# Summing V accumulators through a mask on VectorE and one fp32 matmul, instead of a chain of eight

## The chip, the core and the metric

One core of a Trainium2 chip. The metric is the device time of one execution in microseconds (us).

Engine names: PE is the matmul engine, PEld its weight loads, DVE is VectorE, ACT is ScalarE, SP is the engine that issues the loads. "DMA engines" are the core's 16 engines that carry data.

## The reference

One query token attends to 65,536 keys, with 32 query heads and 8 key/value heads (4 query heads share one, which the kernel calls a group), head size 128, bf16:

```python
B, Hq, Hkv, Sq, Sk, D = 1, 32, 8, 1, 65536, 128
# q [B,Hq,Sq,D], k and v [B,Hkv,Sk,D], all normal * 0.05
k = jnp.repeat(k, Hq // Hkv, axis=1); v = jnp.repeat(v, Hq // Hkv, axis=1)
scores = jnp.einsum("bhqd,bhkd->bhqk", q, k) * D ** -0.5
p = softmax(scores)
return jnp.einsum("bhqk,bhkd->bhqd", p, v)
```

K and V together are 268.4 MB, every byte of which is read once.

## The kernel before

SP loads 64 tiles of 4 MB (128 partitions of 32 KB each) through five buffers, K of the next group in turn with V of the current one. For K, DVE transposes a tile and PE multiplies it with the query. For V, one accumulator row block serves four column slots, so that a matmul can be 32 columns by 512:

```python
def v_step(g, j):
    vt = load(v_view[g, j], "vt")
    # ... A = two PSUM accumulators of [128, 512] fp32, E = exp(scores), transposed
    for c0 in range(0, CW, NQ):
        for u in range(2):
            for s in range(NQ):
                c = c0 + s
                nc.tensor.matmul(out=A[u][s * QP:(s + 1) * QP, :], lhsT=E[:, j, c, :],
                                 rhs=vt_v[:, u, c, :, :], start=..., stop=...)
```

Most of A is not wanted: of each 32 rows, only the four of the block that belongs to the column's slot i (the "diagonal") count. The old kernel copies A to SBUF and gathers the diagonal blocks with fp32 matmuls against columns of a selection matrix:

```python
def collect(g, stop):
    A = A_tiles.pop(g)
    # ... As[0] <- A[0] on ACT, As[1] <- A[1] on DVE
    for i in range(NI):                                   # NI = 8
        nc.tensor.matmul(out=ps_f, lhsT=sel[:, i * HPG:(i + 1) * HPG],
                         rhs=As[i // HI][:, i % HI, :], start=(i == 0), stop=...)
```

The trace records 16 fp32 matmuls per group for these eight calls, two for each. The very last V tile is loaded in five pieces (1/2, 1/4, 1/8, 1/16, 1/16) and multiplied slot by slot in a narrow form (4 by 128), so that little work is left when its last piece lands:

```python
ps_f = collect(g, False)
for t in range(EDGE):                                      # EDGE = 120 of 128 slots
    s = t % NQ
    slot(t, Dp[s * QP:s * QP + HPG, :], t < NQ, t >= EDGE - NQ)
nc.vector.tensor_copy(out=Ds, in_=Dp)
for t in range(EDGE, T):                                   # the last 8 slots
    slot(t, ps_f[:, :], False, False)
nc.tensor.matmul(out=ps_f, lhsT=selh, rhs=Ds, start=False, stop=True)
store(g, ps_f, nc.sync)                                    # o = ps_f / sum, then the store
```

## Time and profile before

| | before |
|---|---|
| device time, median of 3 | 635.4 us (635.21 to 635.79) |
| span of the profiled run | 633.2 us |
| bytes loaded, mean rate | 268.4 MB, 425 GB/s |
| busy: PE, DVE, ACT | 62%, 54%, 4% |
| matmul records on PE | 2314 |
| last load landed, then to the end | 629.63 us, 3.6 us |

The first view is the page of the profiled run: the share of time in which the 16 DMA engines are busy and the rate, in 40 slices of the span; then the DMA queues with packets, megabytes and share of the engines' time.

```profile
DMA  8999999999999999999999999999999999999995
GB/s 366 433 433 436 435 432 433 430 433 427 439 427 433 431 430 431 432 433 431 430 429 430 431 432 431 430 431 431 432 431 430 431 434 433 432 431 431 430 423 233
...
q1 hardware_dynamic: 9800, 268.44, 98.7%
q8 instruction: 18, 0.29, 0.2%
```

The DMA engines are at 90% or more in nearly every slice, and the rate stands at about 430 GB/s until the last two slices (423 and 233). The second queue, 18 packets with 0.2% of the engines' time, carries the instructions of an engine's program.

The second view is the end of the chain of waits (start, duration, what):

```profile
598.94 30.69 DMA vt<-in_v_dram
...
629.68 0.67 PE ps_f L239 x8
630.34 0.44 PE ps_f L252 x2
...
630.81 0.34 DVE o L226
```

One load is waited for until 629.63 us. Eight slots, one matmul and the scaling of the output follow.

The third view is the table of stretches (start:end, length, busy time and count of PE, PEld, DVE, ACT and POOL, the granted clock of PE, DMA share, GB/s).

```profile
624.00:625.00 1.00, 1.00 (x12) 0.80 (x10) 0.07 (x1) 0.00 (x0) 0.00 (x0) 1.00 0.87 348
625.00:626.00 1.00, 1.00 (x60) 0.92 (x57) 0.00 (x0) 0.00 (x0) 0.00 (x0) 1.00 0.55 225
626.00:627.00 1.00, 0.44 (x25) 0.31 (x15) 0.00 (x0) 0.00 (x0) 0.00 (x0) 1.00 0.56 219
627.00:628.00 1.00, 0.62 (x32) 0.47 (x32) 0.00 (x0) 0.00 (x0) 0.00 (x0) 1.00 0.41 154
628.00:628.50 0.50, 0.13 (x12) 0.13 (x15) 0.00 (x0) 0.00 (x0) 0.00 (x0) 1.00 0.06 25
628.50:629.00 0.50, 0.26 (x16) 0.12 (x9) 0.00 (x0) 0.00 (x0) 0.00 (x0) 1.00 0.18 57
```

The fourth view is the timeline of the last tile (start, busy time, engine, line, operation, count, idle time before it and who ended that):

```profile
625.28 1.16 PE L239 MATMUL Dp<-vt,E 128*4 128x128 bf16 x58
627.11 0.62 PE L239 MATMUL Dp<-vt,E 128*4 128x128 bf16 x32 [0.67 <-DMA vt<-in_v_dram]
...
628.37 0.40 PE L239 MATMUL Dp<-vt,E 128*4 128x128 bf16 x16 [0.64 <-DMA vt<-in_v_dram]
...
629.68 0.67 PE L239 MATMUL ps_f<-vt,E 128*4 128x128 bf16 x8 [0.36 <-DMA vt<-in_v_dram]
```

PE has done the first half of the tile at 626.44 (625.28 + 1.16) and waits for each later piece.

### The profile page before, as it was taken

What the parts mean: (1) busy time and instruction counts of PE and PEld (TensorE: products, weight loads), DVE (VectorE), ACT (ScalarE), POOL (GpSimd) and SP (SyncE); (2) the same over time, 40 slices, a digit from 0 to 9 for tenths busy, and PEclk for the clock granted to TensorE, in tenths of its full rate; (3) what the DMA queues carried; (4) which work ended last, traced back from release to release, by engine and by line L of the source; (5) the groups of instructions that cost most, each with busy time, mean ns of one, the idle gap of its engine ahead of it and who ended that gap; (6) DMA issues with size and microseconds to landing.
All of it is one profiled execution on the core that took longest, in us unless ns stands there. A gap on an engine that the chain in (4) does not pass through costs nothing.

```text
span 633.2 us, 5208 instructions
## 1 busy us (share of the span) xinstructions
PE 395.6 (62%) x2314; PEld 158.3 (25%) x2314; DVE 341.7 (54%) x214; ACT 22.4 (4%) x25; POOL 4.9 (1%) x7
## 2 busy tenths in 40 slices
PE   0586776767457675587744777557774568654735
PEld 0232222222122221233211232122331223211313
DVE  0898663765437663466633666345754466553600
ACT  0000100010000100001000000001000010000100
POOL 3000000000000000000000000000000000000000
PEclk9999699758887588885868858688586898777977
DMA  8999999999999999999999999999999999999995
GB/s 366 433 433 436 435 432 433 430 433 427 439 427 433 431 430 431 432 433 431 430 429 430 431 432 431 430 431 431 432 431 430 431 434 433 432 431 431 430 423 233
DMA packets 10070, 268.81 MB, mean 425 GB/s; under 512 B 1344, under 2 KB 1344, under 8 KB 1728
## 3 DMA queue, kind: packets, MB, share of 16 engines
q1 hardware_dynamic: 9800, 268.44, 98.7%
q8 instruction: 18, 0.29, 0.2%
q10 hardware_dynamic: 248, 0.04, 0.0%
q14 instruction: 4, 0.03, 0.0%
HBM read 268.47 MB, written 0.01 MB: 424 GB/s over the span
## 4 chain that ended last, share of the span: by engine, by line
DMA 58%; PE 22%; DVE 15%; issue 5%; ACT 0%; ACTq 0%; DVEq 0%
DMA kt<-in_k_dram 44%; PE S L137 16%; DMA vt<-in_v_dram 12%; DVE kT L128 12%; DMA q_85<-in_q_dram 2%; PE ps_f L217 2%; DVE mx L148 2%; ACT ET L168 0%; PE ps_b L163 0%; DVE Z L112 0%; DVE o L226 0%; PE ps_t L150 0%; PE A_357 L201 0%; PE A_356 L201 0%; ACTq L77 0%
## 5 line engine op out<-in xcount | busy, mean ns | idle before, releaser
L137 PE MATMUL S<-kT,Z 128*128 128x512 bf16 x1024 | 296.7, 448 | 184.6 <-DVE kT L128 184.4
L128 DVE STREAM_TRANSPOSE kT<-kt 128x2048 int32<-128x2048 int32 x128 | 289.6, 2293 | 196.0 <-DMA kt<-in_k_dram 152.2
L137 PEld LDWEIGHTS <-Z 128*128 128x128 bf16 x1024 | 111.6, 109 | 368.3 <-issue 294.4
L201 PEld LDWEIGHTS <-E 128*32 128x32 bf16 x992 | 26.3, 100 | 48.7 <-issue 28.5
L173 DVE STREAM_TRANSPOSE E<-ET 128x2048 bf16<-128x2048 bf16 x8 | 18.5, 2311 | 17.4 <-ACT ET L168 17.4
L148 DVE TENSOR_REDUCE mx<-S 128x1 f32<-128x2048 f32 x8 | 18.3, 2292 | 15.9 <-PE S L137 15.9
L168 ACT ACTIVATE ET<-S,nm 128x2048 bf16<-128x2048 f32 x8 | 15.7, 1967 | 77.8 <-DVE nm L165 77.8
L201 PE MATMUL A_2721<-vt,E 128*32 128x512 bf16 x48 | 8.0, 584 | 12.0 <-DMA vt<-in_v_dram 12.0
L176 PE MATMUL ps_l<-ls,selh 128*4 128x1 f32 x16 | 1.5, 165 | 19.2 <-ACT ET L168 19.2
L214 DVE COPY As_2832<-A_2722 128x512 f32<-128x512 f32 x1 | 0.7, 693 | 21.0 <-PE A_2722 L201 21.0
L163 PE MATMUL ps_b<-one,mrow 1*128 1x1 f32 x16 | 3.2, 269 | 10.7 <-DVE mrow L157 10.7
L102 DVE STREAM_TRANSPOSE qT<-q_85 128x64 int32<-128x64 int32 x1 | 0.2, 245 | 16.0 <-DMA q_85<-in_q_dram 16.0
L226 DVE TENSOR_SCALAR o<-ps_f,rl 4x128 bf16<-4x128 f32 x8 | 2.7, 339 | 9.9 <-PE ps_f L217 8.8
L201 PE MATMUL A_2722<-vt,E 128*32 128x512 bf16 x48 | 7.9, 584 | 0.0
L201 PE MATMUL A_357<-vt,E 128*32 128x512 bf16 x64 | 7.1, 380 | 0.0
L201 PE MATMUL A_356<-vt,E 128*32 128x512 bf16 x64 | 6.9, 382 | 0.0
L201 PE MATMUL A_1045<-vt,E 128*32 128x512 bf16 x64 | 6.6, 380 | 0.0
L201 PE MATMUL A_2421<-vt,E 128*32 128x512 bf16 x64 | 6.6, 380 | 0.0
L201 PE MATMUL A_1733<-vt,E 128*32 128x512 bf16 x64 | 6.6, 380 | 0.0
L201 PE MATMUL A_701<-vt,E 128*32 128x512 bf16 x64 | 6.6, 380 | 0.0
L201 PE MATMUL A_1389<-vt,E 128*32 128x512 bf16 x64 | 6.6, 380 | 0.0
L201 PE MATMUL A_2077<-vt,E 128*32 128x512 bf16 x64 | 6.6, 380 | 0.0
(95 smaller groups left out, 119.1 us busy)
## 6 DMA issues: line engine op xcount, KB each, us to landing
kt<-in_k_dram SPq DMA_DIRECT2D x32, 4096.0 KB, 42.4
vt<-in_v_dram SPq DMA_DIRECT2D x31, 4096.0 KB, 37.8
vt<-in_v_dram SPq DMA_DIRECT2D x1, 2048.0 KB
vt<-in_v_dram SPq DMA_DIRECT2D x1, 1024.0 KB
vt<-in_v_dram SPq DMA_DIRECT2D x1, 512.0 KB
vt<-in_v_dram SPq DMA_DIRECT2D x2, 256.0 KB
out_dram<-o ACTq DMA_DIRECT2D x7, 1.0 KB
q_85<-in_q_dram ACTq DMA_DIRECT2D x4, 8.0 KB, 6.1
```

Of the source, the lines that this page charges most:

```text
L102: nc.vector.transpose(out=qT[:, :].bitcast(i32), in_=q4[:, :].bitcast(i32))
L128: nc.vector.transpose(out=kT[:, :].bitcast(i32), in_=kt[:, i2 * CW * D:(i2 + 2) * CW * D].bitcast(i32),)
L137: nc.tensor.matmul(out=S[:, j, :NCOL], lhsT=Z[:, b, e, g, w0:w0 + P], rhs=kT_v[:, i - i2, b, e, :, :], start=(i == 0 and be == 0), stop=(i ...
L148: nc.vector.reduce_max(out=mx[:, :], in_=S[:, :, :NCOL], axis=AX.XY)
L163: nc.tensor.matmul(out=ps_b[:, :], lhsT=mrow[:, :], rhs=one[:, :], start=True, stop=True)
L168: nc.scalar.activation(out=ET[:, :].rearrange("p (a n) -> p a n", a=NQ), in_=S[:, :, :NCOL], func=ACT.Exp, bias=nm[:, :], scale=SCALE, acc ...
L173: nc.vector.transpose(out=E[:, :, :, :].rearrange("p a c r -> p (a c r)"), in_=ET[:, :])
L176: nc.tensor.matmul(out=ps_l[:, :], lhsT=selh[:, :], rhs=ls[:, :], start=True, stop=True)
L201: nc.tensor.matmul(out=A[u][s * QP:(s + 1) * QP, :], lhsT=E[:, j, c, :], rhs=vt_v[:, u, c, :, :], start=(j == 0 and c0 == 0), stop=(j == e ...
L214: nc.vector.tensor_copy(out=As[1][:, :, :].rearrange("p i d -> p (i d)"), in_=A[1][:, :])
L217: nc.tensor.matmul(out=ps_f[:, :], lhsT=sel[:, i * HPG:(i + 1) * HPG], rhs=As[i // HI][:, i % HI, :], start=(i == 0), stop=(stop and i == ...
L226: nc.vector.tensor_scalar_mul(out=o[:, :], in0=ps_f[:, :], scalar1=rl_tiles.pop(g)[:, :])
```

## The change

The intent is to take the collection from PE and ACT. A mask of zeros and ones, multiplied onto A on DVE, keeps only the diagonal blocks; a reduction over the eight blocks sums them; the sum of exponentials is put beside the result as column 129, so that one fp32 matmul per group does both sums over partitions. The first half of the last V tile is multiplied in the wide form (16 matmuls instead of 64), since it lands early. The core of the diff:

```diff
-        ls = stats.tile([P, 1], fp32, name="ls")
+        R = rpool.tile([P, D + 1], fp32, name="R")
...
-            func=ACT.Exp, bias=nm[:, :], scale=SCALE, accum_out=ls[:, :],
+            func=ACT.Exp, bias=nm[:, :], scale=SCALE, accum_out=R[:, D:],
...
-        ps_l = ... one fp32 matmul for the sums, and a reciprocal
...
-    def collect(g, stop):        # copies of A on ACT and DVE, eight fp32 matmul calls
+    def diagonal(parts, out):
+        n = len(parts) * HI
+        t = apool.tile([P, NI, D], fp32, name="t", tag="t")
+        for x, (u, acc) in enumerate(parts):
+            nc.vector.tensor_tensor(
+                out=t[:, x * HI:(x + 1) * HI, :],
+                in0=acc[:, :].rearrange("p (i d) -> p i d", i=HI),
+                in1=mask[:, u * HI:(u + 1) * HI, None].to_broadcast([P, HI, D]),
+                op=ALU.mult,
+            )
+        nc.vector.tensor_reduce(
+            out=out, in_=t[:, :n, :].rearrange("p i d -> p d i"), axis=AX.X, op=ALU.add,
+        )
...
+    def finish(g):
+        R = R_tiles.pop(g)
+        diagonal(list(enumerate(A_tiles.pop(g))), R[:, :D])
+        ps_f = psm.tile([HPG, D + 1], fp32, name="ps_f", tag="misc")
+        nc.tensor.matmul(out=ps_f[:, :], lhsT=selh[:, :], rhs=R[:, :], start=True, stop=True)
...
     def last_step(g, j):
...
+        W = pss.tile([P, HI * D], fp32, name="W", tag="S")
+        first = halves(vt, 1)[0]
+        for c0 in range(0, CW, NQ):
+            wide(W, E, j, first, 0, c0, start=(c0 == 0), stop=(c0 == CW - NQ))
+        Rw = stats.tile([P, D], fp32, name="Rw")
+        diagonal([(0, W)], Rw[:, :])
+        nc.vector.tensor_add(out=Rw[:, :], in0=Rw[:, :], in1=R[:, :D])
...
-        for t in range(EDGE):
+        for t in range(CUTS[0], EDGE):
...
-        nc.vector.tensor_copy(out=Ds[:, :], in_=Dp[:, :])
+        nc.vector.tensor_add(out=Ds[:, :], in0=Dp[:, :], in1=Rw[:, :])
```

## The prediction

> **What bounds the kernel now.** The load queue. In the slices of the span the DMA engines are at 9 tenths in 39 of 40, and the table of stretches gives a DMA share of 1.00 at 430 to 431 GB/s from 20 to 600 us. 268.4 MB at that rate are 623 of the 633.2 us. [...] PE is busy 62%, DVE 54%. A load is issued 33 to 46 us before it lands (views of tiles kt and vt), so an engine must fall far behind before the stream notices.

> **The tail.** The chain of waits is one load from 598.94 to 629.63, then 8 slot matmuls 0.67 us, the selh matmul to 630.78, o 0.34 us, the store issued at 631.17, and the end. Only these 3.6 us can be shortened by computing differently.

> **Removed.** Per group: the 16 fp32 matmuls of the collection (1.0 to 1.9 us per eight), the copies of As on ACT (0.58) and DVE (0.69). In the last tile: 64 narrow matmuls (1.4 us, 625.06 to 626.44).

> **Added.** Per group two masked multiplies of 128x512 from PSUM. [...] 0.69 us each, the same as the copy here. Then a reduction of 1024 elements: that of 2048 took 2.29 us, so I estimate 1.2. Together 2.6 us against 0.69: DVE gains 1.9 us per group, 15 us in all (342 to about 357 busy). exp starts about 2 us later, but the next K transpose no longer stands behind an o that waits for sixteen matmuls. DVE has slack (105 of 200 us busy between 300 and 500), and the load queue absorbs it.

> In the last tile: 16 wide matmuls (0.9 to 1.8 us)[...].

> **On the critical path?** In the old tail PE had finished the tile's first half at 626.44 and waited 0.67 us for the third quarter, and again for each later piece (0.64, 0.28, 0.36). What it saves before 627.11 is idle time. In the new tail A's diagonal runs on DVE from about 623.3 to 626; W is complete by 626 to 627.1, its diagonal and sum by 627.6 to 628.8; the addition into Ds needs the slots' result at 629.37 as before and is not delayed. The order of instructions ends as before: 8 slots, selh matmul, o, store. Gain: none; loss: none.

> **Predicted time:** 635.4 us, 8 in 10 between 634.7 and 636.2. Chances: faster by over 2% 0.01, within 2% 0.98, slower 0.01.

> **Right or wrong by the profile.** DMA share 1.00 at 430 to 431 GB/s in the middle; last landing at 629.6 +- 0.5; from there to the end 3.5 to 3.7 us; DVE busy up by 12 to 18 us; some 170 matmuls fewer; ACT down by about 5 us; PE waits for DMA before the third quarter; Ds within 0.4 us of the last Dp slot.

> **What would make it wrong.** W's diagonal later than 629.3 ([...] a late first half), which delays the selh matmul and adds up to 1 us; or a change in the stream's rate, which no computation here should cause. Both stay well within 2%.

The 2.6 us per group are twice 0.69 us, which is what the copy of 128x512 took (L214 in the trace before), and the 1.2 us estimated for the reduction. The DVE terms for the last tile came to about 1.6 us, which leads from W, complete by 626 to 627.1, to its sum by 627.6 to 628.8. The 0.9 to 1.8 us for sixteen wide matmuls is an estimate that fits the trace before: groups of four begin 0.22 us apart at 592 us (granted clock 1.00) and 0.43 us apart at 609 us (0.50). The predicted 635.4 us are the median of the kernel before with no gain and no loss; of what is cut, only the conclusion about the stream bears on it.

## The result, and the profile after

| | before | after |
|---|---|---|
| device time, median of 6 | 635.06 us (634.71 to 635.79) | 633.93 us (633.17 to 634.24) |
| ratio | 1 | 0.9978 (95%: 0.9966 to 0.9991) |
| span of the profiled run | 633.2 us | 632.4 us |
| last load landed, then to the end | 629.63, 3.6 us | 628.48, 3.9 us |
| matmul records on PE | 2314 | 2138 |
| busy: PE, DVE, ACT | 395.6, 341.7, 22.4 us | 374.1, 361.7, 17.8 us |

A ratio here is the mean time of one kernel's fast runs over that of the other's of the same rounds, so it is not quite the ratio of the two medians. The change is faster by 0.2%, which is small but clear of the noise: the slowest of its six runs (634.24) is under the fastest of the six before (634.71). The predicted range, 634.7 to 636.2, does not hold it.

The chain of waits after, to be read against that of before:

```profile
599.17 29.32 DMA vt<-in_v_dram
...
628.53 1.01 PE ps_f L271 x8
629.54 0.44 PE ps_f L283 x2
...
630.01 0.34 DVE o L234
```

The last landing is 1.15 us earlier (628.48 against 629.63). What follows it is not shorter: the same eight slots took 1.01 us instead of 0.67, because in this run's tail the granted clock of PE was 0.50; before, it was 1.00 until about 630 us. So the whole gain comes from the loads, in a kernel whose loads were not changed: the same 64 tiles in the same order and pieces, and at the end even issued 0.2 us later (599.17 against 598.94).

The queues after, as the page has them (packets, megabytes, share of the engines' time):

```profile
q1 hardware_dynamic: 9800, 268.44, 98.9%
q8 instruction: 17, 0.28, 0.2%
```

The stretches at the end, after:

```profile
625.00:626.00 1.00, 0.43 (x7) 0.00 (x1) 0.64 (x2) 0.00 (x0) 0.00 (x0) 0.50 0.54 221
...
627.00:628.00 1.00, 0.73 (x28) 0.50 (x23) 0.55 (x2) 0.00 (x0) 0.00 (x0) 0.50 0.39 148
628.00:628.50 0.50, 0.27 (x8) 0.00 (x0) 0.18 (x1) 0.00 (x0) 0.00 (x0) 0.50 0.00 0
628.50:629.00 0.50, 0.47 (x5) 0.47 (x6) 0.11 (x1) 0.00 (x0) 0.00 (x0) 0.50 0.15 33
```

The loads move the same bytes in the same packets. The queue of instructions has 17 packets instead of 18. As before, part of the engines end at about 625 us, the others by 628, but the stretch in which one engine loads alone (0.06) is gone. The 0.15 at 628.5 comes after the last landing.

The tail's timeline after (start, busy time, engine, line, operation, idle time before it):

```profile
626.00 1.02 PE L271 MATMUL Dp<-vt,E 128*4 128x128 bf16 x32 [0.57 <-DMA vt<-in_v_dram]
...
627.30 0.29 DVE L267 TENSOR_TENSOR Rw<-Rw,R 128x128 f32<-128x128 f32 x1
...
628.32 0.29 DVE L280 TENSOR_TENSOR Ds<-Dp,Rw 128x128 f32<-128x128 f32 x1 [0.73 <-PE Dp L271]
...
628.53 1.01 PE L271 MATMUL ps_f<-vt,E 128*4 128x128 bf16 x8 [0.26 <-DMA vt<-in_v_dram]
```

The groups of instructions of the new code on DVE (count, busy time in all, mean ns of one):

```profile
L222 DVE TENSOR_TENSOR t<-A,mask 128x512 f32<-128x512 f32 x16 | 10.8, 680 | 19.4 <-PE A L192 19.4
...
L228 DVE TENSOR_REDUCE R<-t 128x128 f32<-128x1024 f32 x8 | 15.0, 1881 | 0.0
...
L228 DVE TENSOR_REDUCE Rw<-t 128x128 f32<-128x512 f32 x1 | 1.1, 1061 | 0.0
```

DVE has its sum (Rw, ready at 627.59) before the slots end, so this part went as predicted. The masked multiply takes 0.68 us, and the reduction of 1024 elements 1.88 us, half as long again as estimated.

### Reading the packets

The trace also records every DMA packet, without naming its engine. Two things can be read from it. First, when the blocks of the second queue (q8) were fetched: each is 16,384 bytes; before, 17 of them fell into the stream and took 1.02 to 1.10 us each (an 18th came in the last half microsecond), after it is 16 and one after the last landing. Second, how far the 16 engines lie apart: every load ends with one 4-byte record from each engine, and these 16 records, sorted, give the lag of each engine behind the first. The table is worked out from these records for single loads of the kernel before (us; times are those of the packet records, which start 11.0 us ahead of the span; the last column says what the two instruction queues fetched since the line above: 16 KB blocks in q8, 8 KB blocks in another one, q14):

```
load done   lag of the 16 DMA engines behind the first, sorted                       fetched since
  52.7      0.0 0.1 0.1 0.1 0.1 0.1 0.2 0.2 0.2 0.2 0.2 0.2 0.3 0.3 0.4 0.4
  63.7      0.0 0.1 0.1 0.1 0.1 0.1 0.2 0.2 0.2 0.2 0.2 0.3 0.3 0.4 0.4 1.7          one 16 KB block
 102.6      0.0 0.1 0.1 0.1 0.1 0.2 0.2 0.2 0.2 0.3 0.3 0.4 0.4 1.2 1.7 1.7          one 16 KB, one 8 KB
 316.5      0.0 0.1 0.1 0.2 0.2 0.2 0.4 1.2 1.6 1.6 1.7 1.7 1.8 1.8 1.9 1.9          six 16 KB
 356.7      0.0 0.1 0.1 0.2 0.2 0.2 0.4 1.6 1.6 1.7 1.8 1.8 1.8 1.9 2.2 3.2          one 16 KB, one 8 KB
 599.8      0.0 0.2 0.2 0.2 0.2 0.4 0.8 1.8 2.2 3.1 3.1 3.2 3.3 3.3 3.4 3.5          six 16 KB, one 8 KB
 630.2      0.0 0.2 0.2 0.2 0.3 0.4 0.8 3.1 3.1 3.2 3.3 3.3 3.4 3.4 3.4 4.8          two 16 KB, one 8 KB
```

The lags only grow, and they grow in steps. Thirteen 16 KB blocks of this run that fell alone between two loads raised the sum of the lags by 1.50 to 1.66 us each, in each case on one engine. The records also show how such a step is made up: directly after each of the 17 blocks (within 0.02 us of its end) one 32 KB packet of the data took 1.68 to 1.76 us instead of 1.21 to 1.23, so the block costs its own 1.02 to 1.10 us and another half microsecond. The first eight blocks go to eight different engines, the ninth (before 356.7) goes to one that has had one already. The times that the blocks took repeat with a period of eight (1.07, 1.07, 1.07, 1.10, 1.10, 1.09 or 1.10, 1.02, 1.02 us, twice, and then 1.08), which fits a fixed turn. The 8 KB blocks of q14 cost about 1.0 us each (0.89 and 1.01 where one fell alone), on a ninth engine, but for one (between 356.7 and 599.8) that moved a tenth from 0.1 to 0.8. The six other engines never fall behind (0.0 to 0.4 us in the last row). The last row is the last whole tile, after the 17th block: one engine stands at 4.8 us. In the kernel after, the largest lag of that tile is 3.6 us. The difference, 1.12 us before rounding, is nearly the whole 1.15 us by which the last landing moved. How many instructions a block holds is shown by the runs below: 256, 1792 and 2560 PE instructions more add one, seven and ten packets to q8 (17 after; 18, 24 and 27), so 256 each.

### The profile page after: what moved, and what is told of

It is laid out like the page before. It is cut to its first block, busy times and chain, and to the rows that moved or that the text cites. A ratio compares the mean times of both kernels' runs of the same rounds, so it can differ in the third digit from the quotient of the medians.

```text
span 632.4 us, 4867 instructions
## 1 busy us (share of the span) xinstructions
PE 374.1 (59%) x2138; PEld 143.4 (23%) x2138; DVE 361.7 (57%) x234; ACT 17.8 (3%) x17; POOL 4.9 (1%) x7
## 4 chain that ended last, share of the span: by engine, by line
DMA 58%; DVE 18%; PE 18%; issue 4%; ACT 0%; ACTq 0%; DVEq 0%
DMA kt<-in_k_dram 44%; PE S L143 15%; DVE kT L134 12%; DMA vt<-in_v_dram 11%; DMA q<-in_q_dram 2%; PE A L192 2%; DVE mx L154 2%; DVE E L179 1%; DVE R L228 1%; DVE t L222 1%; ACT ET L174 0%; PE ps_f L241 0%; DVE o L234 0%; DVE Z L118 0%; ACTq L235 0%
## 5 line engine op out<-in xcount | busy, mean ns | idle before, releaser
L192 PE MATMUL A<-vt,E 128*32 128x512 bf16 x992 | 66.4, 399 | 12.2 <-DMA vt<-in_v_dram 10.0
L222 DVE TENSOR_TENSOR t<-A,mask 128x512 f32<-128x512 f32 x16 | 10.8, 680 | 19.4 <-PE A L192 19.4
L228 DVE TENSOR_REDUCE R<-t 128x128 f32<-128x1024 f32 x8 | 15.0, 1881 | 0.0
L241 PE MATMUL ps_f<-R,selh 128*4 128x129 f32 x14 | 3.7, 362 | 10.2 <-DVE nm L171 10.2
L156 PE MATMUL ps_t<-ident,mx 128*1 128x128 f32 x8 | 2.2, 270 | 6.3 <-DVE mx L154 6.3
L169 PEld LDWEIGHTS ps_b<-one,mrow 1*128 1x128 f32 x16 | 2.6, 199 | 13.4 <-PE A L192 7.7
L112 POOL MEMSET Z<- 128x4992 bf16 x1 | 4.3, 4264 | 0.0
L271 PEld LDWEIGHTS <-E 128*4 128x4 bf16 x64 | 2.2, 111 | 2.5 <-issue 2.0
L192 PE MATMUL W<-vt,E 128*32 128x512 bf16 x16 | 1.9, 625 | 1.3 <-DMA vt<-in_v_dram 1.3
```

The costliest lines, as they stand in the source:

```text
L112: nc.gpsimd.memset(Z[:, :, :, :, :], 0.0)
L156: nc.tensor.transpose(out=ps_t[:, :], in_=mx[:, :], identity=ident[:, :])
L169: nc.tensor.matmul(out=ps_b[:, :], lhsT=mrow[:, :], rhs=one[:, :], start=True, stop=True)
L192: nc.tensor.matmul(out=dst[s * QP:(s + 1) * QP, :], lhsT=E[:, j, c0 + s, :], rhs=v_half[:, :, c0 + s, :], start=start, stop=stop,)
L222: nc.vector.tensor_tensor(out=t[:, x * HI:(x + 1) * HI, :], in0=acc[:, :].rearrange("p (i d) -> p i d", i=HI), in1=mask[:, u * HI:(u + 1) ...
L228: nc.vector.tensor_reduce(out=out, in_=t[:, :n, :].rearrange("p i d -> p d i"), axis=AX.X, op=ALU.add,)
```

## The experiments

The rivals, as the expectations name them: theory W, less work near the last landing (the wide form); theory C, that the copies and fp32 matmuls had disturbed the loads, so that less traffic speeds the stream; and for the runs about the steps, L (each block costs the stream as much as the first) and S (a block costs only its bytes). Every kernel was timed in five rounds, on one chip together with the kernel before (the three sets of runs were on three chips).

### One block more

In the changed kernel, the 128 K matmuls of group 1 are split in two halves of 256 columns. PE does the same multiplications with 256 more instructions.

```diff
-                    nc.tensor.matmul(out=S[:, j, :NCOL], lhsT=Z[...], rhs=kT_v[:, i - i2, b, e, :, :], ...)
+                    parts = 2 if g == 1 else 1
+                    cw = CW // parts
+                    for h in range(parts):
+                        nc.tensor.matmul(out=S[:, j, h * cw * QP:(h + 1) * cw * QP], lhsT=Z[...],
+                            rhs=kT_v[:, i - i2, b, e, h * cw:(h + 1) * cw, :], ...)
```

> The changed kernel with 128 K matmuls of one early group split in two halves: 256 PE instructions more, nothing else. Theory F (instruction fetch: the 16 KB blocks of PE's program are fetched on 8 of the 16 load engines in turn; the old kernel fetched 17 before its stream ended, so that one engine had three and finished last, the new one 16, two on each): a 17th block falls into the stream, the last landing goes back from 628.5 to about 629.6, and the time is 1.0 to 1.5 us over that of the changed kernel, within 0.4 us of the kernel before (ratio 0.9995 to 1.0005). Theory W (less work after or near the last landing) and theory C (less traffic of ACT and PE disturbs the loads less): time stays that of the changed kernel, ratio about 0.998.

Measured: 635.57 us (635.23 to 635.78), ratio 1.0003 (0.9989 to 1.0016); before 635.31. PE busy was 374.8 us against 374.1. Its queue of instructions, from the page (17 of the 18 packets lie in the stream, the last comes after it):

```profile
q8 instruction: 18, 0.29, 0.2%
```

The stretches of this run:

```profile
627.00:628.00 1.00, 0.43 (x23) 0.39 (x20) 0.88 (x2) 0.00 (x0) 0.00 (x0) 0.50 0.34 131
628.00:628.50 0.50, 0.50 (x24) 0.44 (x17) 0.50 (x1) 0.00 (x0) 0.00 (x0) 0.50 0.06 25
628.50:629.00 0.50, 0.27 (x16) 0.13 (x11) 0.47 (x2) 0.00 (x0) 0.00 (x0) 0.50 0.06 25
629.00:629.50 0.50, 0.46 (x16) 0.27 (x9) 0.20 (x1) 0.00 (x0) 0.00 (x0) 0.50 0.06 25
```

The engine that loads alone is back (0.06), from 628 us on, and the last eight slots start at 630.16. One block more in an early group, far from the tail, gives away the whole gain. Theories W and C fall here: all that they credit is still in this kernel.

### One block less in the kernel before

In the kernel before, half of the K matmuls of two middle groups are left out, 128 in all. This is wrong (the comparison with the reference still let it pass, which says more about its tolerance than about this kernel).

```diff
+                    if g in (3, 4) and be in (1, 2):
+                        continue
                     nc.tensor.matmul(
                         out=S[:, j, :NCOL],
```

> The kernel before, with 128 of its K matmuls in two middle groups left out (wrong result on purpose): 256 PE instructions fewer, collection and tail untouched. Theory F: 16 blocks instead of 17 in the stream, last landing near 628.3, time 1.0 to 1.5 us under the kernel before, ratio 0.9975 to 0.9985. Theories W and C: no change, ratio 1.000 +- 0.0005.

Measured: 633.63 us (633.46 to 634.28), ratio 0.9975 (0.9963 to 0.9988). The end of its chain of waits:

```profile
599.10 29.36 DMA vt<-in_v_dram
...
628.51 0.61 PE ps_f L241 x8
...
629.37 0.34 DVE o L228
```

Its queue of instructions, from the page:

```profile
q8 instruction: 17, 0.28, 0.2%
```

The old collection, the old tail, and yet the last eight slots start at 628.51, as in the changed kernel (628.53). Taking out 256 PE instructions alone is worth as much as the whole change.

### The two parts of the change alone

The wide form alone, in the kernel before (old collection kept; W is masked and summed on DVE as in the change):

```diff
         ps_f = collect(g, False)
+        W = pss.tile([P, HI * D], fp32, name="W", tag="S")
+        ... 16 wide matmuls into W; mask and sum into Rw
-        for t in range(EDGE):
+        for t in range(CUTS[0], EDGE):
...
-        nc.vector.tensor_copy(out=Ds[:, :], in_=Dp[:, :])
+        nc.vector.tensor_add(out=Ds[:, :], in0=Dp[:, :], in1=Rw[:, :])
```

> The kernel before with only the last tile's first half in wide form (old collection kept). The 96 instructions that go are all in the last tile, after the 17th block has been fetched. Theory F: still 17 blocks in the stream, no gain, ratio 1.000 +- 0.0006. Theory W: the gain comes from here, ratio 0.998. Theory C: no gain.

Measured: 635.39 us (634.95 to 636.08), ratio 1.0004 (0.9991 to 1.0017); 2266 matmul records, 17 blocks in the stream. No gain, as theory F expects. (In the kernel before, the 17th block is fetched at 612.8 us of the span, and the narrow matmuls of the last tile start at 625.06.)

The diagonal by mask alone, with the last tile narrow as before:

```diff
-        W = ... 16 wide matmuls, diagonal([(0, W)], Rw), Rw += R
-        for t in range(CUTS[0], EDGE):
+        for t in range(EDGE):
...
-        nc.vector.tensor_add(out=Ds[:, :], in0=Dp[:, :], in1=Rw[:, :])
+        nc.vector.tensor_add(out=Ds[:, :], in0=Dp[:, :], in1=R[:, :D])
```

> The changed kernel with the last tile in the old narrow form throughout (diagonal by mask kept). Theory F: the 17th block[...] is asked for [...] in the third quarter of the last tile (about 627.3), while its engine still has loads to do: the last landing at about 629.2, most of the gain lost, ratio 0.9985 to 1.0000. Theory W: no gain, 1.000. Theory C: the full gain, 0.998.

Measured: 634.08 us (633.23 to 634.27), ratio 0.9979 (0.9966 to 0.9991). My expectation missed. This part takes 2314 - 2186 = 128 matmul records, 256 instructions, which is one block, and it has the full gain. I had expected the 17th block to be fetched at about 627.3, while its engine was still loading, and the last landing at about 629.2. The packet records show the block at 627.6, 0.5 us before the last packet of the stream, and the last landing came at 628.52, as in the changed kernel: the block held nothing up. That its engine had finished by then is likely but not shown, since the records name no engine. The theory stands, but it does not say to a few tenths of a microsecond which block is still in time to do harm. Taken by itself this run would also have suited theory C; the two runs above had already ruled that out.

### The staircase

If eight engines take the blocks in turn, 17 to 24 blocks should all cost the same, and the 25th should cost a further step. The splitting of K matmuls is extended to groups 1 to 7 (seven blocks more, 23 in the stream), and then to V matmuls of three groups (ten more, 26):

```diff
-                    parts = 2 if g == 1 else 1
+                    parts = 2 if g >= 1 else 1
```

> The changed kernel with the K matmuls of seven groups split in two: 1792 PE instructions more, seven blocks, so 23 in the stream. Theory F (8 engines take the blocks in turn, and the one with most of them ends the stream): 17 to 24 blocks are three on the fullest engine, as with one block more; last landing 629.6 to 630.3, time as that of the run with 256 instructions more, 635.0 to 635.8, ratio 0.9995 to 1.0010; about seven engines, not one, still busy in the last microsecond. Rival L (every block costs the stream the same 1.5 us that the first one cost): 644. Rival S (a block only takes its 16 KB out of the 430 GB/s of all engines, 0.04 us): 634.2.

Measured: 635.47 us (634.91 to 635.79), ratio 1.0006 (0.9994 to 1.0019).

```diff
+            n = 2 if split else 1          # split=(g in (2, 3, 4))
+            w = HI // n
+            for h in range(n):
+                nc.tensor.matmul(out=dst[s * QP:(s + 1) * QP, h * w * D:(h + 1) * w * D], ...,
+                    rhs=v_half[:, h * w:(h + 1) * w, c0 + s, :], ...)
```

> As the run before, with V matmuls of three groups split as well: 2560 PE instructions more, ten blocks, 26 in the stream, so two engines have four. Theory F: one more step, 1.0 to 1.6 us over the run with seven blocks, 636.2 to 637.2, ratio 1.0015 to 1.0035. Rival L: 649. Rival S: 634.4.

Measured: 637.01 us (636.81 to 637.13), ratio 1.0032 (1.0019 to 1.0044). The queues of instructions of the two runs, from their pages (in each the last packet comes after the stream):

```profile
q8 instruction: 24, 0.39, 0.3%
...
q8 instruction: 27, 0.44, 0.3%
```

Stretches of the run with 23 blocks:

```profile
628.00:628.50 0.50, 0.50 (x24) 0.42 (x15) 0.50 (x1) 0.00 (x0) 0.00 (x0) 0.52 0.45 172
628.50:629.00 0.50, 0.27 (x19) 0.15 (x15) 0.47 (x2) 0.00 (x0) 0.00 (x0) 1.00 0.49 188
...
629.50:630.00 0.50, 0.28 (x8) 0.10 (x7) 0.17 (x1) 0.00 (x0) 0.00 (x0) 1.00 0.01 4
```

The same of the run with 26 blocks:

```profile
628.50:629.00 0.50, 0.36 (x16) 0.36 (x19) 0.47 (x2) 0.00 (x0) 0.00 (x0) 0.50 0.53 205
...
629.50:630.00 0.50, 0.27 (x16) 0.11 (x11) 0.47 (x2) 0.00 (x0) 0.00 (x0) 0.50 0.13 49
630.00:630.50 0.50, 0.49 (x16) 0.29 (x9) 0.22 (x1) 0.00 (x0) 0.00 (x0) 0.50 0.13 49
```

With 23 blocks seven or eight engines (0.45 to 0.49 of sixteen) load until 629 us instead of one, and the time is that of one block more (ratio 1.0006 against 1.0003, on another chip): six blocks for nothing. With 26 there are two engines left at 630 us (0.13 of sixteen, two engines with four blocks), and the time is 1.5 us higher. Theory L (644 and 649 us) and theory S (634.2 and 634.4 us) both fall.

### Far fewer blocks

The changed kernel with 736 K and 496 V matmuls left out (wrong):

```diff
+                    if be in (1, 2) or (be == 3 and i < NI - 1):
+                        continue
...
-        for c0 in range(0, CW, NQ):
+        for c0 in (0, CW - NQ):
```

> The changed kernel with 736 of its K matmuls and 496 of its V matmuls left out (wrong result on purpose): 2464 PE instructions fewer, 6 or 7 blocks in the stream, so no load engine has more than one. Theory F: one step down from the changed kernel, 1.0 to 1.6 us: last landing 627.0 to 627.5, ratio 0.9950 to 0.9965, eight or nine engines done 1.5 us before the rest instead of 3.1. Rival P (it is PE's idle time or its clock that matters, in proportion to the matmuls left out): ten times the effect of the 128 left out of the kernel before, 15 us. Theories W and C: as the changed kernel or a few tenths under it.

Measured: 633.64 us (633.50 to 633.93), ratio 0.9982 (0.9969 to 0.9994). It missed: the last slots start at 628.01, 0.5 us earlier than in the changed kernel (628.53), not 1.0 to 1.6 us, and the time is 0.5 us under that of the changed kernel in the same rounds (634.16, below). Rival P falls all the same: ten times as many matmuls left out as in the cut of the old kernel, and no more gained. Its queue of instructions, from the page (the seventh packet was fetched in the last microsecond of the stream):

```profile
q8 instruction: 7, 0.11, 0.1%
```

The stretches show what is in the way:

```profile
625.00:626.00 1.00, 0.53 (x24) 0.53 (x27) 0.97 (x2) 0.00 (x0) 0.00 (x0) 0.50 0.44 168
626.00:627.00 1.00, 0.77 (x32) 0.57 (x24) 0.96 (x2) 0.00 (x0) 0.00 (x0) 0.50 0.19 66
627.00:628.00 1.00, 0.71 (x21) 0.23 (x12) 0.23 (x2) 0.00 (x0) 0.00 (x0) 0.50 0.03 12
```

From 626 to 627 us three engines' worth is busy (0.19, with a seventh block of code among it), and after that one for half of the time (0.03). The lags of the last whole tile, from the packet records as above, show the one that is left:

```
              16 KB blocks   lag of the 16 DMA engines behind the first, sorted
before             17        0.0 0.2 0.2 0.2 0.3 0.4 0.8 3.1 3.1 3.2 3.3 3.3 3.4 3.4 3.4 4.8
after              16        0.0 0.0 0.1 0.2 0.2 0.3 0.6 2.9 3.0 3.2 3.2 3.2 3.3 3.3 3.6 3.6
far fewer           6        0.0 0.2 0.3 0.3 0.3 0.3 0.4 0.4 0.7 1.6 1.7 1.7 1.9 2.0 2.3 3.2
```

Six engines stand one step back (1.6 to 2.3), with one block each, as expected. One stands at 3.2 us. It got there in steps of about 1 us at three 8 KB blocks of q14; the last of them moved it from 2.3 to 3.2. I had not counted this ninth engine. It caps what can be gained by fewer PE instructions at about half a microsecond below the changed kernel. Which engine's program these 8 KB blocks belong to was not tried.

### Dealing the rows out unevenly

If the late engines cannot be spared their blocks, they could be given fewer rows. In the trace before, each load of 128 rows ends with sixteen 4-byte records, and the last store, of 4 rows, with four; that a load of 8 rows would go to eight engines, and that they could be the early ones, was assumed. So one V tile was loaded as 112 rows and twice 8 rows. The trace of that run agrees with the number: the two 8-row loads add eight 4-byte records each, 1108 in all against 1092 in the kernel before (on the pages, 9816 packets in q1 against 9800); which engines they are it does not show:

```diff
+        if skew:                                  # one tile: g == 3 and j == 0
+            for lo, hi in ((0, 112), (112, 120), (120, 128)):
+                nc.sync.dma_start(out=t[lo:hi, :], in_=view[lo:hi, :])
+            return t
```

> The changed kernel with one V tile of the middle loaded as 112 rows on all engines and twice 8 rows, which should go to eight engines only. The eight engines without instruction blocks end 3.1 us before the other eight. If the 8-row loads go to those that end early, they get 9 rows of this tile and the others 7: the late eight end 1.2 us earlier, the last landing at about 627.3, time 632.4 to 632.9, ratio 0.9955 to 0.9968. If they go to the late ones, the last landing comes 1.2 us later and the time is 634.8 to 635.3. Theories W and C: as the changed kernel.

> As the run before, with another quarter of a row shifted in another V tile (together 1.25 rows, the two halves of the engines should end within 0.2 us of each other), and the last piece of the last tile halved to 4 slots. If the 8-row loads go to the early engines: last landing about 627.0, 0.2 to 0.4 us less after it, time 631.7 to 632.4, ratio 0.994 to 0.996. If not: 635 or more.

Measured: 649.73 us (649.36 to 651.62; ratio 1.0239, 1.0225 to 1.0252) and, with a second such tile and a smaller last piece, 657.31 us (653.83 to 657.91; 1.0341, 1.0318 to 1.0364). A clear failure: the first took 14.9 us longer than the kernel before in the same rounds (634.88). The rate of the first, in slices of the span:

```profile
GB/s 379 433 425 433 435 424 435 434 425 434 433 427 434 435 424 435 434 348 184 399 425 433 431 431 430 433 428 433 431 430 433 426 435 433 424 436 432 425 428 214
```

The rate drops to 184 GB/s around that one tile. In the packet records most 32 KB packets around that tile took about 2.2 us and the slowest 33, towards its end, about 4, against 1.2 us elsewhere. Why they were slow, and whether the idea could work with another division of the rows, stays open.

### A smaller last piece

To see whether something can still be had after the last landing, the changed kernel was run again, beside one with one cut more, so that 4 slots instead of 8 follow it:

```diff
-    CUTS = (T // 2, 3 * T // 4, 7 * T // 8, T - T // 16)
+    CUTS = (T // 2, 3 * T // 4, 7 * T // 8, T - T // 16, T - T // 32)
```

> The changed kernel again, for a comparison on the same chip: ratio 0.9975 to 0.9985.

> The changed kernel with one cut more in the last tile, so that 4 slots instead of 8 follow the last landing. The 8 slots took 0.61 to 1.01 us by the granted clock. The last landing stays, what follows it gets 0.2 to 0.5 us shorter: 0.2 to 0.5 us under the changed kernel of the same rounds.

Measured: the changed kernel 634.16 us (633.90 to 634.28), ratio 0.9988 (0.9974 to 1.0002), just outside what was expected; here the gain is 0.7 us, and although its slowest run is under the fastest of the kernel before (634.60), the interval reaches 1. With the extra cut 633.65 us (633.43 to 633.97), ratio 0.9981 (0.9969 to 0.9994); before 634.84. The four slots took 0.59 us and the eight 1.01, the time that the eight took at a granted clock of 0.50 in other runs; the clock in these two tails was not read. The last slots began 0.05 us later (628.66 against 628.61). The medians differ by 0.5 us and the ranges overlap a little (633.97 and 633.90). It is the lowest median of the correct versions, but its lead over the changed kernel is not clear of the noise of a few runs. Its ratio to the kernel before is.

### All runs side by side

| kernel | matmul records | 16 KB blocks in the stream | most on one engine | last slots start | median us | ratio to before |
|---|---|---|---|---|---|---|
| before | 2314 | 17 | 3 | 629.68 | 635.06 | 1 |
| wide form alone | 2266 | 17 | 3 | 629.93 | 635.39 | 1.0004 |
| one block more | 2266 | 17 | 3 | 630.16 | 635.57 | 1.0003 |
| seven more | 3034 | 23 | 3 | 630.14 | 635.47 | 1.0006 |
| ten more | 3418 | 26 | 4 | 631.18 | 637.01 | 1.0032 |
| before, cut | 2186 | 16 | 2 | 628.51 | 633.63 | 0.9975 |
| diagonal alone | 2186 | 16 | 2 | 628.56 | 634.08 | 0.9979 |
| after | 2138 | 16 | 2 | 628.53 | 633.93 | 0.9978 |
| after, again | 2138 | 16 | 2 | 628.61 | 634.16 | 0.9988 |
| after, smaller last piece | 2138 | 16 | 2 | 628.66 | 633.65 | 0.9981 |
| after, far fewer | 906 | 6 | 1 | 628.01 | 633.64 | 0.9982 |

The two runs with uneven rows are left out. Blocks that were fetched in the last 1.0 us of the stream are not counted. This limit was drawn after the runs: the cut kernel and the diagonal alone have such a block, and their last landings are those of the changed kernel, which has none. "Most on one engine" is the count divided by eight, rounded up. It sorts the starts of the last slots without exception, and the times but for the last row, where the ninth engine sets the end.

## Why the prediction was right or wrong

**The step that failed** is in the last two sentences of the section on the critical path and in "What would make it wrong": "Gain: none; loss: none", and "a change in the stream's rate, which no computation here should cause". It begins in "The tail": "Only these 3.6 us can be shortened by computing differently." The last landing was expected at 629.6 +- 0.5 and came at 628.48. The prediction treated the stream as one pipe with a rate. It is sixteen engines that end at different times, ten of which had also carried program code, and the last landing moved with the one that carried most (the largest lag is 4.8 us before and 3.6 us after). What PE computed did not matter to it here, but how many instructions PE is told in did: in the kernel before, 256 fewer of them were worth 1.7 us (635.31 to 633.63; 1.16 us of it in the last landing of the profiled runs, 629.63 to 628.47), and in the changed kernel 256 more took the gain away. The conclusion that the stream had nothing left to gain looked at the middle, where the DMA share is 1.00 at 430 to 431 GB/s, and was silent about the end: over the last 4.6 us before the landing (625.0 to 629.6) the DMA share was 0.36 on average, 0.55 at first and 0.06 from 628.0 to 628.5. It was luck that the instructions removed were just enough to drop the block that mattered: nobody had counted blocks.

**What held.** The bound (DMA share 1.00 in the middle, in both kernels); that the savings of PE in the old tail were idle time (the wide form alone gained nothing, 1.0004); that DVE's new work would be absorbed by the queue of loads; that Ds would not be late (628.32, 0.05 us after the last slot); about 170 matmul records fewer (176) and ACT down by about 5 us (4.6); and that the change stays within 2%.

**Sizes that were off.** The reduction over the blocks took 1.88 us instead of the estimated 1.2, so DVE gained 20.0 us instead of 12 to 18; this lies off the critical path. The sum over the blocks reads a strided view (128 sums of 8 elements, 512 bytes apart): 1024 elements took 1.88 us and 512 took 1.06, against 2.29 us for 2048 in the maximum over scores. Whether the stride or the many outputs make it slower was not separated. From the last landing to the end it took 3.9 us instead of 3.5 to 3.7, because PE had half the clock: at a granted clock of 0.50 the last eight slots took 1.01 us (after, and one and ten blocks more), at 1.00 they took 0.61 (the cut kernel, and seven blocks more); before, where it fell from 1.00 to 0.50 during them, 0.67. This gave back 0.3 us of the profiled run's gain of 1.15. Why the clock is granted so was not tried.

**Still open.** Why the data packet directly after a block takes half a microsecond longer, and why only eight of the sixteen engines carry PE's blocks.

## What to carry to other kernels

In a kernel bound by loads, look at the last few microseconds of the stream by the share of DMA engines that are busy. Here it was 0.55 and then 0.06: the engines ended apart, and the last one set the time. In this kernel the unrolled program was loaded by the same engines as the data, so the count of instructions was a cost even on an engine that was busy for 62%; it came in steps of 8 blocks of 256 PE instructions, 1.1 to 1.7 us of time each (0.5 us for the step from 16 blocks to 6, where another engine set the end), so a gain or loss of this size after an unrelated edit should be checked against the number of packets in the instruction queue before anything else is believed. And a part of a change that "does nothing" on the critical path may still have been the one that brought the gain, for a reason that nobody intended.
